# Last batch's second halves written by rows from TensorE, more scaling steps free to change engine, and the whole hand-written order replaced

## Chip, core and metric

The kernel runs on one core of one Trainium2 chip. The metric is the device time of one execution in microseconds (us); the median of the runs is compared. The engines are named as in the profile: PE is TensorE's matmul, PEld its weight load, DVE is VectorE, ACT is ScalarE, POOL is GpSimd, SP is SyncE, which here only issues DMAs. A "q" behind an engine's name means its instruction queue, where DMAs are issued.

## What is computed

The reference has two stages over 8 batches of 576 tokens and 512 channels (8 heads of 64), all in float32:

```python
k_p = k.reshape(B, H, Sp, 8, D).mean(axis=3); v_p = v.reshape(B, H, Sp, 8, D).mean(axis=3)
scores = scale * np.matmul(q, k_p.transpose(0, 1, 3, 2))
attn = exp(scores - max) / (sum + 1e-09)
x = np.matmul(attn, v_p)                       # then heads side by side: (8, 576, 512)
theta = x @ w_theta
y = einsum('ts,bsd->btd', w_tok_r, x * cos(theta)) + einsum('ts,bsd->btd', w_tok_i, x * sin(theta))
u = x + y
out = u + maximum(u @ w_ch, 0.0)
```

The four weight matrices arrive as 64-bit floats (two 32-bit words a number) and are put together on the chip.

## The kernel before, in words

One core does all eight batches. The work is cut into small generators ("streams"), and each `yield` ends a step. A stream's name has a letter for its kind, then the batch, then a part:

- `k`, `v` load keys and values, `K`, `V` pool them, `Q` loads and turns the queries.
- `S b.m` (`soften`, L696) makes the softmax of token tile m: four or eight matmuls (L715, L723), a maximum on DVE, the exponential on ACT (L766 for batches 0 and 1, L778 for the others), the sum and its reciprocal, and then the scaled copy `en` of `e`: one product of 128x512 (L785) and one of 128x64 (L792), on DVE or POOL. POOL takes a product of 512 or more columns in two halves (L172 to L193). From batch 2 on DVE then transposes `en` into `G` (L801, L804), and `E` (`turn`, L856) moves its blocks with 16 DMAs and splits the result in a high and a low part.
- `X` (`attend`, L893) multiplies with the values and copies the result from PSUM into `xT` (L921 on ACT, L923 on DVE).
- `T b.m` (`rotate`, L947) makes theta, its sine and cosine, and the products with x; its cast `xh` (a copy, L204 for ACT, L206 for DVE and POOL) goes to any of three engines.
- `h`, `w`, `c` make the weights. Their words are turned into floats by `to_f32` (L345): the scaled high words always on ACT (L353), the low words on a chosen engine (L357, L359).
- `Z` (`take`, L1013) splits z, and `M b.c.hf` (`mix`, L1034) does the token mixing of channel chunk c and token half hf (288 tokens): 27 matmuls (L1047) in three groups, an addition on DVE (L1057), the cast `uh` (L204, L206) and the low part `ul` (L189 POOL, L1064 DVE).
- `F b.c.hf` (`final`, L1070) is the end of a chunk and half: 12 matmuls (L1080) into a bank `pf`, then `max(.,0)` plus u on DVE (L1087), then a DVE transpose in 32x32 blocks into `R` (L1100), and DMAs to the output. Batches 0 to 6 issue four DMAs a chunk on SP (L1115). Batch 7 issues four DMAs for each of its eight parts (L1105), alternately on ACT's queue and on SP's, from the tile `rz`. Each of these DMAs writes pieces of 32 channels, 128 bytes.

The order is written out by hand: `SCHEDULE` (L30 to L136) is a list of 2064 words. Each word runs one step of the stream that it names (L1198 to L1201), and a letter at its end (v DVE, g POOL, a ACT) is the engine that `pick()` gives in that step. Every engine, and every DMA queue, executes its own instructions in the order in which the words issue them; an engine whose next instruction waits for another engine lets nothing overtake. PSUM has four one-bank buffers for most matmul groups (`bank`, L234) and two double ones. All DMAs of the two queues share eight completion semaphores, and a DMA waits until the earlier one on its semaphore has landed.

At the end of the list PE does the mixing of batch 7, and then the eight `F7` parts one behind the other.

Of the kernel before, what the change touches and what calls it, by code (L numbers as in the profile page):

```python
# [134 lines left out]
F7.1.1 F7.2.0 F7.2.0 F7.0.1 F7.0.1 F7.0.1  # L135
"""  # L136

EARLY, EXACT, V_ON_PE, K_ON_PE, Q_ON_PE, SUMS_ON_ACT = 2, 1, 1, 1, 2, 2


@with_exitstack
def tile_attn_moe(
    ctx: ExitStack,
    tc: tile.TileContext,
# [86 lines left out]
    def bank(shape, name):  # L234
        return ps.tile(shape, F32, tag="mm", name=name, bufs=4)
# [1001 lines left out]
```

## Time and profile before

| what | value |
|---|---|
| median of 3 runs | 571.96 us (570.99 to 573.55) |
| profiled execution, its time | 572.55 us |
| profiled execution, its span from the first to the last instruction | 570.5 us |
| instructions | 11555 |
| mean granted TensorE clock | 0.997 |
| busy: PE, DVE, POOL, ACT | 96%, 80%, 63%, 55% of the span |
| DMA | 57.84 MB, mean 101 GB/s |

The profile page is one profiled execution. Busy time is the union of an engine's instructions; issuing a DMA is not counted as busy. A group's line gives busy time and the mean of one instruction, and behind the bar the idle time of that engine just before these instructions with what ended it. The chain of waits follows the last instruction back to what released it, step by step.

### The profile page before, as it was taken

To read this page: it belongs to the slowest core of one execution; us is meant where nothing else is said; L and a number is where in the kernel's file an instruction comes from. 1 tells how busy PE (TensorE), PEld (TensorE's weight loads), DVE (VectorE), ACT (ScalarE), POOL (GpSimd) and SP (SyncE) were. 2 spreads that over 40 slices of the span, in tenths; PEclk is the share of its full clock that TensorE was granted. 3 is DMA by queue.
4 is the path that set the end of the run, shared out by engine and by line. 5 is a ranking of instruction groups with operands and counts; after the bars stand their busy time and mean duration, and the time that the engine had idled before them with its cause. 6 is when DMAs were issued, how large, how long until landed. Compare 5 with 4: busy or idle time off the path is not lost.

```text
span 570.5 us, 11555 instructions
## 1 busy us (share of the span) xinstructions
PE 546.7 (96%) x4072; PEld 512.9 (90%) x4072; DVE 456.3 (80%) x875; ACT 313.3 (55%) x673; POOL 361.8 (63%) x518
## 2 busy tenths in 40 slices
PE   6999989999999999999999999999999999999993
PEld 5776879998989898999999999999999999999993
DVE  4998998989889999978897997779878775655452
ACT  2999998878554587455417655349225473242000
POOL 3324565687584897648884997838777878522610
PEclk9999999999999999999999999999999999999998
DMA  9995321556676666556565564656234341200225
GB/s 263 270 310 125 81 67 64 120 119 97 131 126 117 127 97 116 105 117 121 109 119 103 84 116 83 122 94 89 41 66 84 66 68 24 44 1 1 43 38 88
DMA packets 235385, 57.84 MB, mean 101 GB/s; under 512 B 223424, under 2 KB 223936, under 8 KB 235328
## 3 DMA queue, kind: packets, MB, share of 16 engines
q1 hardware_dynamic: 230464, 56.52, 50.0%
q10 hardware_dynamic: 4864, 0.59, 0.7%
q8 instruction: 32, 0.52, 0.4%
q14 instruction: 25, 0.20, 0.1%
HBM read 37.81 MB, written 9.44 MB: 83 GB/s over the span
## 4 chain that ended last, share of the span: by engine, by line
PE 65%; DVE 17%; DMA 5%; SPq 5%; POOL 3%; issue 2%; ACT 2%; DVEq 0%; POOLq 0%; ACTq 0%
PE py L1047 27%; PE pf L1080 13%; PE pt L959 11%; PE pv L912 4%; PE s L723 3%; SPq L867 3%; PE px L973 2%; DMA kpst<-in_k_dram 2%; DMA vpst<-in_v_dram 2%; DVE G L801 1%; SPq L603 1%; PE kpp L570 1%; DMA qsst<-in_q_dram 1%; DVE R L1100 1%; DVE en L785 1%
## 5 line engine op out<-in xcount | busy, mean ns | idle before, releaser
L1047 PE MATMUL py<-WTh,zh 128*128 128x288 f32 x576 | 81.9, 288 | 2.8 <-POOL zh L206 2.1
L1047 PE MATMUL py<-WTl,zh 128*128 128x288 f32 x576 | 81.8, 287 | 0.0
L1047 PE MATMUL py<-WTh,zl 128*128 128x288 f32 x576 | 81.3, 289 | 0.2
L1047 PEld LDWEIGHTS py<-WTh,zh 128*128 128x128 f32 x576 | 74.6, 189 | 3.9 <-POOL zh L206 2.3
L1047 PEld LDWEIGHTS py<-WTl,zh 128*128 128x128 f32 x576 | 75.3, 189 | 0.2
L1047 PEld LDWEIGHTS py<-WTh,zl 128*128 128x128 f32 x576 | 74.3, 189 | 1.2 <-DVE zl L1031 0.3
L189 POOL TENSOR_TENSOR zl<-z,zh 128x256 fp32r<-128x256 f32 (+2 forms) x77 | 60.6, 816 | 19.2 <-DVE zh L206 13.5
L189 POOL TENSOR_TENSOR en<-e_eps,ri 128x256 f32<-128x256 f32 (+3 forms) x61 | 34.5, 583 | 48.6 <-DVE ri L782 36.5
L965 ACT ACTIVATE g<-pt,c_magic 128x512 f32<-128x512 f32 x35 | 24.1, 687 | 50.9 <-PE pt L959 34.7
L1057 DVE TENSOR_TENSOR xT<-py,xT 128x288 f32<-128x288 f32 x64 | 27.9, 443 | 25.9 <-PE py L1047 25.6
L1080 PE MATMUL pf<-uh,chh 128*128 128x288 f32 x256 | 43.5, 293 | 1.4 <-DVE xT L923 0.9
L1080 PE MATMUL pf<-ul,chh 128*128 128x288 f32 x256 | 42.1, 286 | 0.2 <-POOL ul L189 0.2
L189 POOL TENSOR_TENSOR ul<-xT,uh 128x288 fp32r<-128x288 f32 x39 | 32.1, 832 | 15.8 <-DVE uh L206 15.5
L1080 PE MATMUL pf<-uh,chl 128*128 128x288 f32 x256 | 41.8, 286 | 0.0
L189 POOL TENSOR_TENSOR xl<-xT,xh 128x256 fp32r<-128x256 f32 x38 | 30.2, 818 | 16.8 <-ACT xh L204 12.5
L1087 DVE SCALAR_TENSOR_TENSOR xT<-pf,xT 128x288 f32<-128x288 f32 x64 | 27.9, 444 | 15.9 <-PE pf L1080 15.6
L778 ACT ACTIVATE e_eps<-e_eps 128x576 f32<-128x576 f32 (+1 forms) x30 | 20.6, 685 | 36.5 <-DVE e_eps L774 36.3
L959 PE MATMUL pt<-th,xh 128*128 128x512 f32 x148 | 39.2, 388 | 0.9 <-ACT xh L204 0.8
L1080 PEld LDWEIGHTS pf<-uh,chh 128*128 128x128 f32 x256 | 36.0, 189 | 2.9 <-DVE xT L923 1.2
L959 PE MATMUL pt<-th,xl 128*128 128x512 f32 x148 | 38.1, 380 | 0.0
L959 PE MATMUL pt<-tl,xh 128*128 128x512 f32 x148 | 38.0, 379 | 0.0
L921 ACT ACTIVATE xT<-pv 128x320 f32<-128x320 f32 (+1 forms) x41 | 15.8, 407 | 38.6 <-PE pv L912 31.1
(259 smaller groups left out, 1441.6 us busy)
## 6 DMA issues: line engine op xcount, KB each, us to landing
out_dram<-R SPq DMA_DIRECT2D x112, 72.0 KB, 2.1
kpst<-in_k_dram SPq DMA_DIRECT2D x15, 512.0 KB, 4.2
vpst<-in_v_dram SPq DMA_DIRECT2D x28, 256.0 KB, 4.0
qsst<-in_q_dram SPq DMA_DIRECT2D x96, 72.0 KB, 2.9
eraw<-G SPq DMA_DIRECT2D x96, 60.0 KB, 2.2
eraw<-G SPq DMA_DIRECT2D x96, 40.0 KB, 2.0
WTh_st<-in_moe_w_theta_dram SPq DMA_DIRECT2D x4, 512.0 KB, 7.5
wcraw<-in_moe_w_ch_dram SPq DMA_DIRECT2D x4, 512.0 KB, 3.5
```

What stands on the lines that cost most here:

```text
L189: nc.gpsimd.tensor_tensor(out[:, r], a[:, r], b[:, r], op)
L723: nc.tensor.matmul(scs[c // 2][:n, 2 * SP * (c % 2) : 2 * SP * (c % 2 + 1)], qT[:, c, t0 : t0 + n], kpT[:, c, :], start=True, stop=True,)
L778: nc.scalar.activation(e[:n], e[:n], AF.Exp, scale=scale)
L867: nc.sync.dma_start(blocks(Ex, jj, i), blocks(Gx, i, jj))
L912: nc.tensor.matmul(as_written(pv[:, :gn]) if pair else pv[:, :gn], l, by_turns(r) if pair else r, start=i == 0, stop=i == len(terms) - 1,)
L921: nc.scalar.activation(x, pv, AF.Copy, scale=1.0 / POOL)
L959: nc.tensor.matmul(as_written(pt), l[:, c, :], by_turns(r[:, c, :]), start=i == 0, stop=i == 11)
L965: nc.scalar.activation(halves(g), in_order(pt), AF.Identity, bias=c_magic)
L1047: nc.tensor.matmul(as_written(py[:, :n]), l[:, kk, :], by_turns(r[:, kk, t]), start=i == 0, stop=i == 3 * NK - 1,)
L1057: nc.vector.tensor_tensor(halves(u), in_order(py[:, :n]), halves(u), ALU.add)
L1080: nc.tensor.matmul(as_written(pv[:, :n]), l[:, kk, o], by_turns(uhl[r][:, kk, t]), start=i == 0, stop=i == 11,)
L1087: nc.vector.scalar_tensor_tensor(halves(oT), in_order(pv[:, :n]), 0.0, halves(oT), ALU.max, ALU.add)
```

## The change

Three functions and the list of words change.

**final.** For batch 7 and the second token half (`BY_ROWS = 1`) the DVE transpose and the four DMAs are gone. In their place PE transposes the 128x288 result in three pieces into a new bank `po` of 96 rows by 3x128, two copies (engine by letter) bring 96x256 and 96x128 to the tile `rows`, and two DMAs write them, in whole rows of 128 channels (512 bytes): the first on SP, the second on SP too, but on ACT's queue for chunk 0. The four DMAs of each first half are now all on ACT's queue.

**soften.** With letter a the large product of `en` is done by eight ACT instructions of 64 columns, each with a scale from `ri` (one number a partition).

**to_f32.** The scaled high words may go to DVE or POOL as well.

```diff
-        nc.scalar.activation(t, hi.bitcast(F32), AF.Copy, scale=2.0**-112)
+        if pick() == "a":
+            nc.scalar.activation(t, hi.bitcast(F32), AF.Copy, scale=2.0**-112)
+        else:
+            ENG[pick()].tensor_scalar(t, hi.bitcast(F32), 2.0**-112, None, ALU.mult)
...
+        if pick() == "a":
+            for h in range(8):
+                nc.scalar.activation(
+                    en[:n, GM * h : GM * h + GM], e[:n, h, 0:GM], AF.Copy, scale=ri[:n, h : h + 1]
+                )
+        else:
+            ENG[pick()].tensor_tensor(
...
+            if hf == BY_ROWS:
+                w = n // 3
+                po = bank([P, 3, P], f"po{c}_{hf}")
+                for j in range(3):
+                    nc.tensor.transpose(po[:w, j], xT[:, c, t0 + w * j : t0 + w * j + w], ident)
+                yield
+                rows = Rs["rows"][:w, c]
+                copy(pick(), rows[:, 0:2], po[:w, 0:2])
+                yield
+                copy(pick(), rows[:, 2], po[:w, 2])
+                yield
+                to = out[b, t, o].rearrange("(j p) a -> p j a", p=w)
+                nc.sync.dma_start(to[:, 0:2], rows[:, 0:2])
+                (nc.sync if c else nc.scalar).dma_start(to[:, 2], rows[:, 2])
+                yield
+                return
...
-                (nc.scalar if i % 2 else nc.sync).dma_start(
+                nc.scalar.dma_start(
```

**SCHEDULE.** All words stand in a new order (2072 of them: the four second halves of batch 7 have two more each), and many letters differ. The ends of the two lists:

```diff
-F7.0.0 M7.2.1v M7.1.1 M7.1.1g M7.1.1v M7.3.1 F7.0.0 F7.3.0 F7.3.0 F7.3.0 M7.3.1g F7.3.0 F7.1.0 F7.1.0 M7.3.1g F7.3.1
-F7.2.1 F7.1.0 F7.0.0 F7.1.1 F7.2.1 F7.3.1 F7.2.1 F7.1.0 F7.2.0 F7.1.1 F7.3.1 F7.1.1 F7.0.0 F7.2.1 F7.2.0 F7.3.1 F7.0.1
-F7.1.1 F7.2.0 F7.2.0 F7.0.1 F7.0.1 F7.0.1
...
+M7.0.1g F7.0.0 F6.0.1 M7.3.1a F7.3.0 M7.3.1g F6.3.1 F7.3.0 F7.1.0 F7.0.0 F7.1.0 F7.2.0 F7.1.0 F7.1.0 F7.2.0 F7.3.1
+F7.2.0 F7.2.0 F7.3.1 F7.1.1 F7.3.1 F7.3.1v F7.3.1v F7.3.1 F7.1.1 F7.2.1 F7.1.1 F7.1.1v F7.1.1v F7.1.1 F7.2.1 F7.0.1
+F7.2.1 F7.2.1v F7.2.1v F7.2.1 F7.0.1 F7.0.1 F7.0.1v F7.0.1v F7.0.1
```

In the new list PE's last groups are, in order: the matmuls of F7.0.0, F7.3.0, F7.1.0, F7.2.0, F7.3.1, F7.1.1, the transposes of F7.3.1, the matmuls of F7.2.1, the transposes of F7.1.1, the matmuls of F7.0.1, the transposes of F7.2.1, and those of F7.0.1. All eight copies of the second halves are on DVE.

How many steps of a kind have each engine, before and after:

| step | DVE | POOL | ACT |
|---|---|---|---|
| large product of `en` (40) | 20, then 15 | 20, then 10 | 0, then 15 |
| cast `uh` (64) | 20, then 18 | 24, then 15 | 20, then 31 |
| low part `ul` (64) | 25, then 22 | 39, then 42 | none |
| cast `xh` (40) | 10, then 7 | 14, then 15 | 16, then 18 |
| high words of the weights (17) | 0, then 5 | none | 17, then 12 |
| copy of `pv` into `xT` (64) | 23, then 21 | none | 41, then 43 |

Read along the words, ACT's exponentials and its sines take turns 34 times in the list before, 30 times in the new one. Matmuls and weight loads of batches 0 to 6 are the same in number and shape.

## Rows read from the trace of the kernel before

**Rows 1.** The page's first part: span, and busy time of each engine.
```profile
span 570.5 us, 11555 instructions
PE 546.7 (96%) x4072; PEld 512.9 (90%) x4072; DVE 456.3 (80%) x875; ACT 313.3 (55%) x673; POOL 361.8 (63%) x518
```

**Rows 2.** Stretches: length, busy PE, PEld, DVE, ACT, POOL; granted clock, DMA share, GB/s.
```profile
0.00:20.00 20.00, 14.78 (x106) 13.60 (x107) 10.70 (x24) 9.84 (x29) 6.16 (x13) 1.00 0.97 285
150.00:200.00 50.00, 46.84 (x358) 44.21 (x359) 45.37 (x86) 25.43 (x45) 32.99 (x44) 1.00 0.69 123
200.00:250.00 50.00, 49.05 (x363) 47.03 (x362) 45.96 (x83) 28.76 (x49) 36.60 (x56) 1.00 0.58 105
300.00:350.00 50.00, 50.00 (x371) 48.50 (x370) 42.38 (x80) 30.16 (x52) 39.11 (x58) 1.00 0.54 102
562.00:570.50 8.50, 0.00 (x0) 0.00 (x0) 0.72 (x2) 0.00 (x0) 0.00 (x0) 0.79 0.56 83
```

**Rows 3.** Waits of PE and PEld: us in total, times, longest us.
```profile
PE kpp L570 <- POOL chh_st L322: 4.6, 1, 4.6
...
PE py L1047 <- POOL zh L206: 2.1, 1, 2.1
...
PEld pv L912 <- ACT xT L921: 2.3, 3, 1.4
```

**Rows 4.** Chain of waits: shares by engine; its last stretch of PE (start, length).
```profile
PE 65%; DVE 17%; DMA 5%; SPq 5%; POOL 3%; issue 2%; ACT 2%; DVEq 0%; POOLq 0%; ACTq 0%
...
549.99 11.77 PE pf L1080 x96
```

**Rows 5.** Issues of line L1105 (min/median/max ns, first and last start), then landing.
```profile
L1105 ACTq DMA_DIRECT2D out_dram<-rz x16: 322/440/478, 554.0 to 563.2; - x16
L1105 SPq DMA_DIRECT2D out_dram<-rz x16: 316/405/472, 558.9 to 568.0; - x16
...
DMA to landing us min/median/max: 1.6/1.7/2.0
```

**Rows 6.** Prices for the end: groups by form, a piece of the chain, one line.
```profile
L1087 DVE SCALAR_TENSOR_TENSOR xT<-pf,xT 128x288 f32<-128x288 f32 x64 | 27.9, 444 | 15.9 <-PE pf L1080 15.6
L923 DVE TENSOR_SCALAR xT<-pv 128x256 f32<-128x256 f32 x12 | 4.8, 416 | 2.9 <-PE pv L912 2.7
...
509.77 0.44 PE px L973 x4
...
L206 DVE COPY kp<-kpp x2: 273/282/292, 8.4 to 12.8; 128x128 f32<-128x128 f32 x2
```

**Rows 7.** Prices for the steps that change engine: groups by line and form.
```profile
L785 DVE TENSOR_TENSOR en<-e_eps,ri 128x512 f32<-128x512 f32 x16 | 13.0, 812 | 0.4
L189 POOL TENSOR_TENSOR en<-e_eps,ri 128x256 f32<-128x256 f32 x28 | 18.0, 666 | 14.3 <-DVE ri L782 8.6 <-DVE mx L757 5.6
L766 ACT ACTIVATE e_eps<-s,mx 128x72 f32<-128x72 f32 x48 | 14.6, 338 | 0.0
L674 ACT COPY vrx<-vrh 32x64 f32<-32x64 f32 x14 | 3.4, 244 | 0.3
L204 ACT CAST uh<-xT 128x288 fp32r<-128x288 f32 x20 | 8.1, 426 | 0.6 <-DVE xT L1057 0.3
L206 POOL CAST uh<-xT 128x288 fp32r<-128x288 f32 x24 | 12.1, 512 | 8.3 <-DVE xT L1057 8.2
L189 POOL TENSOR_TENSOR ul<-xT,uh 128x288 fp32r<-128x288 f32 x39 | 32.1, 832 | 15.8 <-DVE uh L206 15.5
L1064 DVE TENSOR_TENSOR ul<-xT,uh 128x288 fp32r<-128x288 f32 x25 | 14.9, 607 | 0.5 <-POOL uh L206 0.5
L206 DVE CAST xh<-xT 128x512 fp32r<-128x512 f32 x8 | 5.1, 636 | 0.6 <-ACT xT L921 0.5
L353 ACT ACTIVATE wsrc_a<-wraw 128x576 f32<-128x576 f32 x7 | 5.4, 768 | 3.6 <-DMA wraw<-in_moe_w_tok_r_dram 3.5
L359 DVE TENSOR_SCALAR wsrc_b<-wraw 128x576 fp32r<-128x576 uint32 x3 | 1.6, 537 | 0.0
L980 ACT ACT_TABLE_LOAD x16 | 20.5, 1283 | 0.3
```

More of the change, by code (lines that the diff above doesn't have):

```diff
@@ new lines @@
+Q0.0a K0a h1v K0 h1a h1v Q0.1 h0 h1 K0a S0.0 Q0.4 S0.0 Q0.1 Q0.2 h1 Q0.4 w0.1 S0.0 h0g Q0.1a h1g Q0.3 Q0.4v h0 Q0.2v
+w0.1v h0v w0.1g h2 k1.0 S0.1 h0 S0.1 h3 h1 Q0.3 S0.2 S0.0 S0.1 Q0.3v v0.2 h2a D h2v w0.1v S0.1 h2a S0.0 S0.0v S0.0g
+w0.1 S0.3 S0.2 v0.0 S0.1 S0.0 S0.2 K1.0g h1v h1 S0.0v v0.1 S0.1g h3a V0.2 S0.3 h2 w0.1 S0.4 w1.1 h2 S0.0 S0.2 S0.2
+w1.0 S0.3 h3a S0.0v h3v k1.1 S0.1g V0.0 h2v S0.2v S0.3 S0.1 w0.0 S0.2g V0.1 w3.1 S0.1a h3 w2.0 h3 w0.0v w1.1a w3.0
+S0.1 w1.0a S0.1v S0.3 S0.4 w1.0a w0.1g h2 w1.1a w1.0a W0 h2v V0v V0 h2 w1.1a S0.4 Q1.1 S0.2 S0.2a w1.0 X0.0.0 X0.0.1
@@ new lines @@
+T0.2a W1 T0.3a Q1.2 T0.1 W2 Q1.3 w3.1v Q1.2v w4.0v T0.3v V1a c0 T0.2v w4.0a w4.0a T0.1 w4.0 w3.0v Q1.3a T0.2 w4.0 W2a
+Q1.4 X0.2.3g T0.2 T0.1 T0.3 T0.2 W2 c0a c0a T0.2 c0 T0.4g T0.4g T0.2 T0.3 T0.2a w4.0g W3 T0.2 T0.4 W3a T0.3 c0 T0.2
+T0.3 c0 T0.3 T0.2 T0.3a K1 W2 W3 T0.4 T0.4 K1a T0.4 Q1.4 c1 T0.4 c0g W2v T0.3 c0g c0g W2 W4 V1g T0.4 T0.3 c1a T0.4
+T0.3 c1a S1.0 Z0.1a Z0.0g W4v S1.0 k2.2 W4 c1 M0.1.0 Z0.1v c1 K2.2v W4a M0.1.0 M0.0.0 c1 W4 S1.0 W4a S1.0 M0.1.0
+M0.0.0 W4 c2 c1g W4v S1.1 c1g S1.0a W4 Q1.4v c1v W3 W3a Z0.0v W3 M0.1.1 M0.1.1 c2a M0.1.0 S1.0v S1.1 v1.2 M0.0.1 S1.0
@@ new lines @@
+M0.3.1 T1.1g k2.1 Q2.0 S1.3 M0.3.0 T1.0 M0.3.0 S1.3v K2.1g M0.3.1 S1.4 S1.3 M0.2.1a M0.0.1g S1.3 K2 T1.0 M0.2.0g Q2.1
+M0.0.0g M0.3.0 S1.3v T1.0 K2a T1.0a S1.4g T1.0 T1.0 T1.1 S1.3 S1.4v M0.2.1g S1.4 S1.4a T1.0 S1.4 S1.4 M0.1.0g S1.4a
+S1.4 K2 v2.0 V2.0g K2v X1.2.1 T1.1 X1.2.0 X1.2.0a M0.3.0a Q2.1 T1.1 X1.2.2 M0.3.1g X1.2.1a Q2.1 X1.2.3 T1.1 T1.1
+X1.2.2v v2.1 X1.2.3a T1.1v M0.3.0g S2.0 T1.2a S2.0 Q3.0 T1.1 Q3.0 M0.0.1v T1.1 T1.3a T1.2g T1.1 S2.0 V2.1v M0.3.1g
+S2.1 T1.2 S2.2 S2.0 F0.0.1 X1.2.3g T1.2 T1.2 F0.0.1 S2.0g T1.2 S2.0g T1.2 F0.0.0 k3.0 S2.1 S2.1 S2.0 F0.1.0 T1.2a
@@ new lines @@
+S2.3 v3.2 X2.0.0 S2.4 Z1.2g M1.1.0 S2.4 S2.4a Q3.1 V3.0g M1.1.1 M1.0.1 S2.4g X2.0.1 X2.0.1a Q3.1 X2.0.2 V3.2g S3.2
+X2.0.3 S2.4 X2.0.2v Z1.3a X2.0.0a M1.2.0 M1.1.1a M1.3.0 Z1.2g S3.2 S3.2 M1.1.0 F0.3.1 X2.0.3a T2.0a T2.1g S3.2 S3.3
+M1.2.1 M1.2.0 v3.1 M1.0.1a T2.0v S3.2a M1.2.0 Z1.3v E2.2 S3.2v M1.2.0 T2.0 V3.1g M1.2.1 M1.3.0 S3.3 M1.1.0g M1.3.0
+E2.2 M1.2.0v T2.0 S3.3 M1.0.0a M1.3.1 S3.4 T2.1v T2.0 M1.1.0g E2.2 E2.2 T2.0 S3.3 M1.3.1 T2.0 F0.2.1 E2.2a M1.3.0
+T2.0a S3.2 E2.2g k4.0 E2.2g S3.3v S3.3g T2.0 T2.1 M1.2.0g S3.4 E2.2g Q4.0 S3.3 Q4.0 T2.0 k4.2 M1.3.1 S3.4 T2.0 S3.4
@@ new lines @@
+M2.1.1 S4.1a S4.1g X3.0.1a M2.0.0a M2.3.0 M2.3.0 Z2.2a V4.1g S4.1 X3.0.3 Z2.2g X3.0.2 X3.0.3a M2.1.1 S4.2 X3.0.2v
+M2.1.1a S4.2 M2.3.0 T3.0a T3.0g M2.3.1 M2.0.0v M2.3.1 S4.2 M2.1.1v M2.3.1 T3.1a S4.4 V4a T3.0 M2.3.1 k5.0 S4.2g E4.0
+M2.3.0 S4.3 M2.2.1 T3.1g M2.2.0 M2.3.1a E4.0 K5.0v T3.0 S4.2g M2.2.0 T3.2a V4.2g T3.0 M2.3.0a M2.0.1a S4.3 Q5.0 E4.0
+S4.3 M2.1.0g M2.2.1 k5.1 M2.2.0 E4.0 T3.0 k5.2 F1.3.1 T3.2v T3.0 M2.2.1 S4.3 V4g T3.0a Q5.1 S4.2 M2.3.0g T3.0 M2.2.1
+M2.2.1v K5.1g M2.1.0v T3.0 M2.2.0 M2.2.1g v5.0 T3.0 T3.1 T3.4g M2.0.1v Q5.1 K5 V4 T3.1 M2.2.0g T3.1 K5v V4g E4.0g
@@ new lines @@
+F1.2.1 T3.2 T3.1 T3.3a T3.1 K5.2g T3.3g T3.1a M2.3.1v T3.1 F2.1.1 T3.1 T3.1 T3.2 M2.2.0g E4.0a E4.0g F2.1.1 T3.2
+F2.0.1 F2.0.1 F2.1.0 T3.2 T3.2 F2.2.0 Q5.1 T3.2a T3.2 F2.1.0 v5.2 Q6.0 T3.3 S4.3v T3.2 S4.3g K5 T3.2 F2.1.0 F2.0.0
+F2.2.0 S4.4 V5.0g Q6.0 T3.3 F2.1.1 K5a T3.3 T3.3 F2.3.1 T3.3 T3.3a F2.0.0 F2.0.1 T3.3 F2.3.0 S4.4 V4g v5.1 T3.3 E4.0g
+T3.3 Z3.0g F2.2.1 F2.1.1 F2.3.1 Z3.0g F2.0.0 V5.2g F2.0.1 F2.3.0 F2.2.1 M3.0.0 S5.2 F2.3.0 S4.3 X4.0.1 M3.0.1 M3.0.0
+S4.4 S4.4v F2.3.1 F2.2.1 S4.4v F2.2.0 Z3.2a X4.0.0 X4.0.0a S4.4 Z3.2g S5.2 M3.0.1 M3.0.1 V5.1g X4.0.1a X4.0.2 S5.2
@@ new lines @@
+E5.2 T4.0 M3.2.1v M3.2.0g M3.3.0 M3.0.0v T4.0v T4.0 M3.3.1v S5.0 T4.1g M3.0.1v M3.3.0 T4.1 T4.0 M3.3.0v T4.0 M3.1.1g
+M3.3.0g K6 S5.0 T4.1 M3.3.1g F3.0.0 F3.3.0 T4.2v T4.2g X4.2.3g V5a T4.3a T4.1 S5.0 T4.1 S5.0g T4.1 F3.0.0 T4.1a K6v
+F3.3.0 E5.2 E5.2 V5g T4.1 S5.0v Q6.1 T4.1 F3.0.0 V5 T4.1 K6 T4.2 S5.1 E5.2g E5.2g V5v F3.0.1 T4.2 K6v T4.2 F3.1.1
+F3.0.1 F3.1.0 S5.1 T4.3g S5.1 F3.1.0 F3.3.1 F3.0.1 F3.2.1 S5.0 v6.0 F3.3.1 F3.1.1 T4.2 F3.1.0 E5.2g T4.2 V5g T4.2a
+E5.2g T4.3 T4.2 F3.1.1 T4.2 Q6.1 T4.2 X5.2.1 F3.0.1 F3.1.1 T4.3 F3.3.1 S5.1a F3.3.0 Q6.1 S5.1g F3.2.1 T4.3 F3.2.0
@@ new lines @@
+S7.2a M5.1.0 E6.2 V7.0v T6.0a M5.1.0 M5.3.0 V7.2g S7.2v T6.0g M5.1.0 S7.3 M5.0.1v T6.0 S7.3 Z5.2v T6.0 Z5.2v M5.2.0
+T6.1g E6.2 M5.1.0 M5.0.1g T6.0 E6.2 M5.1.1 M5.0.0g E6.2a M5.2.0 E6.2g E6.2g M5.1.0a T6.0 S7.3 T6.0 E6.2v M5.1.0v
+M5.2.1 v7.1 S7.2 T6.0v M5.2.0 T6.0 S7.4 M5.2.1 T6.0 S7.3g F4.2.1 S7.3v M5.2.0 M5.2.0v S7.4 S7.4 M5.3.1 M5.2.1 F4.0.1
+S7.0 T6.0 M5.2.1 X6.2.2 S7.3 M5.2.0g M5.3.0v M5.3.1 X6.2.1 X6.2.1v V7.1g M5.3.1 T6.1g S7.4 M5.2.1g S7.4v X6.2.3
+M5.1.1a S7.4g S7.4 X6.2.2a X6.2.0 T6.1 M5.3.1 M5.3.0v T6.1 X6.2.3a X6.2.0v S7.0 M5.3.1v V7a S7.0 V7g T6.1 F5.1.0 E7.2
@@ new lines @@
+F5.1.0 E7.2 M5.1.1g T6.2g V7 M5.2.1g T6.1 F5.0.0 E7.2 F5.3.0 T6.1 F5.0.0 S7.0 T6.2v T6.3g T6.1a T6.1 F5.1.0 M5.3.1g
+T6.2 F5.0.0 X6.2.3g F5.0.1 F5.3.0 V7g E7.2 F5.1.1 T6.1 T6.1 T6.2 F5.0.1 F5.0.1 F5.0.1 E7.2a T6.2 T6.2 E7.2g F5.1.1
+T6.2 T6.3v F5.2.1 T6.2a F5.2.1 F5.1.1 F5.1.1 T6.3 E7.2g F5.2.0 E7.2g V7v T6.2 F5.2.1 T6.2 T6.2 F5.3.1 F5.2.0 X7.2.2
+F5.2.0 T6.3 T6.3 X7.2.3 F5.3.1 X7.2.1 X7.2.0 F5.3.0 F5.3.1 X7.2.3v T6.3 S7.1 T6.3 X7.2.1v X7.2.2a X7.2.0a T6.3v
+X7.2.3v T6.4v S7.0g T6.3 T6.3 T6.4g T6.3 T6.4 Z6.0g F5.3.1 Z6.0v Z6.0v T6.4 T6.4 T7.3v T6.4 Z6.0g S7.0v T6.4 T6.4a
@@ new lines @@
+T6.4 T6.4 T7.3v M6.0.0 M6.0.1 T6.4 Z6.0a M6.0.0 Z6.0g T7.2a M6.0.1 S7.1 S7.1 M6.0.0 Z6.1g T7.3 M6.0.1 F5.2.1 Z6.1g
+S7.0 M6.0.0 S7.1 S7.1v S7.1g M6.1.0 M6.0.0 M6.0.1 M6.1.0 S7.1 E7.0 M6.1.0 M6.0.0a M6.1.1 M6.1.1 E7.0 M6.1.1 Z6.3g T7.3
+M6.0.1 M6.1.0 M6.3.0 M6.1.1 Z6.3g Z6.2g M6.0.0v M6.3.1 M6.3.0 M6.2.0 M6.2.0 Z6.2v T7.3 E7.0 E7.0 M6.2.0 M6.3.1 T7.2g
+M6.2.0 T7.4g M6.3.1 M6.1.1a M6.3.0 M6.3.0 T7.3 M6.2.1 M6.3.1 T7.3 M6.0.1g T7.3a E7.0a M6.2.1 M6.1.1v E7.0a E7.0v
+M6.2.1 M6.3.1v T7.3 T7.3 M6.2.1 E7.0g M6.2.0a M6.3.1g M6.2.1a T7.2 M6.0.1g X7.0.1 T7.3 X7.0.0 X7.0.1v X7.0.2 T7.2
@@ L136 @@
 """
 EARLY, EXACT, V_ON_PE, K_ON_PE, Q_ON_PE, SUMS_ON_ACT = 2, 1, 1, 1, 2, 2
+BY_ROWS = 1
 @with_exitstack
@@ L784, in soften @@
         en = temp(b, m, "en", 8 * SP)
[L785 to L790 removed]
+        if pick() == "a":
[5 more added lines that the diff above has]
+            ENG[pick()].tensor_tensor(
+                en[:n, 0:512].rearrange("p (h g) -> p h g", h=8),
+                e[:n, :, 0:GM],
+                ri[:n].unsqueeze(2).broadcast_to([n, 8, GM]),
+                ALU.mult,
+            )
         yield
@@ L1094, in final @@
                 Rs["z"] = rz[:, 0 : NC * S].rearrange("p (c s) -> p c s", c=NC)
+                Rs["rows"] = rz[:, NC * S : NC * S + 12 * P].rearrange("p (c j a) -> p c j a", c=4, j=3)
             R = Rs["z"][:, c]
+            if hf == BY_ROWS:
[14 more added lines that the diff above has]
+                return
         else:
```

161 lines of the change are left out of this document (53 added, 108 removed).

## The prediction, made before the changed kernel was run

> **What bounds the kernel now.** I read the page's busy times first, then the stretches, the waits of PE, the chain of waits, and last the DMA issues of the end. The reader is to see in the busy times that PE is the bound: 546.7 of 570.5 us [rows 1]. The 23.8 us that it is not busy are the most that any order of the same work can give back, and they lie in three places. At the start PE's first matmul waits 4.6 us [rows 3]; k0.0 and K0.0 head both lists, so I leave that alone. At the end PE's last group closes at 549.99 + 11.77 = 561.76 us [rows 4], and 8.7 us follow in which it does nothing [rows 1, 2, 4]. What is left, 23.8 - 4.6 - 8.7 = 10.5 us, are short waits in the body, the longest 2.1 us before the first mixing [rows 3]. Most of them lie before 250 us: in 150 to 250 us PE lacks 4.1 of 100 us while DVE is busy for 91% of the time; in 300 to 350 us PE lacks nothing [rows 2]. The chain says the same: 65% PE, 17% DVE, 3% POOL, 2% ACT [rows 4]. So DVE, where it matters, is the engine that PE waits for directly or through others.
>
> **The end, removed part by part.** After the last PE group DVE needs two instructions, but SP issues DMAs of the last batch from 558.9 until 568.0 us, 16 of them, some 0.5 us apart near the end, while ACT's queue has issued its own by 563.2 us [rows 5]. The last lands 1.7 us after its issue, at 569.7, and 0.8 us of closing waits bring the span to 570.5. So the end is bound by SP's queue. The change takes 16 issues of the second halves down to 8 and gives SP 7 of these; the 16 of the first halves go to ACT's queue.
>
> Is ACT's queue late instead? Its first part is F7.3.0. The new list puts six more matmul groups of 1.47 us (11.77 / 8) and six transposes between that part's matmuls and the end of the last group, some 9.5 us; four DVE steps of 0.46 us stand before the first DMA, so it can be issued about 7.6 us before PE's last group ends. Sixteen at 0.5 us are through 0.4 us after that end, ahead of the one issue of F7.0.1, which comes 2.9 us after it. I cost it at nothing; the cover is 2.5 us. SP has by then the eight issues that remain of batch 6 and six of the second halves, and stands free before the last.
>
> **The end, added.** T is the end of the last matmul group. Three transposes take 3 x 0.11 = 0.33 us of PE [rows 6] and end some 0.16 us later, so 0.5 us. Two copies from PSUM cost DVE 0.42 us (by the 128x256 copy) and 0.28 us (by the 128x128 copy) [rows 6]. After T come the transposes of F7.2.1 0.5, its two copies 0.70, the DVE step of F7.0.1 0.44, its transposes 0.5, its copies 0.70, six handovers of some 0.03, the last DMA 1.7 from issue to landing, and the close 0.8: 5.5 us. Before T PE has six transposes more, 0.7 us, with 0.1 us for changing shapes. The end is then 0.8 + 5.5 = 6.3 us instead of 8.7: **-2.4 us**. On the small side, every second half waits on DVE: after a matmul group DVE still has two copies, and then the step of the next part, about 1.8 us against 1.8 us of PE work; if each of two such places loses 0.5 us and the landing takes 2.0 us, -1.1 us is left. On the large side, copies and handovers at half their price give -3.2 us. No row has a landing of 512-byte rows; it takes the 1.6 to 2.0 us of the 128-byte ones [rows 5]. The clock is no term here: it was granted in full to 562 us, and its mean of 0.79 stands in the stretch after PE had stopped [rows 2].
>
> **Steps that change engine.** Fifteen large products of `en` go to ACT, eight instructions each. No row shows one. The nearest is the exponential on 72 columns with a number a partition, 338 ns [rows 7], of which 14.6 / 48 = 0.305 us is its own busy time; a copy of 64 columns without such a number is 244 ns. So a block costs ACT between 8 x 0.244 = 2.0 and 8 x 0.338 = 2.7 us; I take 8 x 0.305 = 2.4, the row nearest in operands, in all 36 us. A block on DVE took 0.81, on POOL 2 x 0.67 = 1.33 us. By the Trainium skill ("ScalarE: Activation LUTs", What ACT_TABLE_LOAD costs), an instruction with one pointer operand takes 280 ns + 0.833 ns a column, and neighbours overlap by 93 ns: an estimate of 8 x 333 - 7 x 93 = 2.0 us a block and 30 us in all, the lower end of my bounds.
>
> - ACT: +36 for `en`, +11 x 0.43 for `uh`, -5 x 0.77 for high words, and four table loads fewer at 1.28 [rows 7]: 36 + 4.7 - 3.8 - 5.1 = +32 us on 313, to 60% of the span. Its idle time hides nearly all of it; 10% on its 2% of the chain is 1.1 us.
> - DVE: -5 x 0.81 for `en`, -3 x 0.61 for `ul`, -2 x 0.5 for `uh`, -3 x 0.64 for `xh`, +5 x 0.54 for high words [rows 7]: -6.1 us on 456, 1.3%, and of its 17% of the chain (97 us) -1.3 us.
> - POOL: -10 x 1.33, -9 x 0.51, +3 x 0.83 [rows 7]: -15 us on 362, 4%; on 3% of the chain (17 us) -0.7 us.
>
> Together **-0.9 us** in the body. The unlettered rest is small in number, and I leave it out. The redrawn order moves loads and DMA issues past others on SP's queue too; of PE's longest waits none in the body names a DMA [rows 3], so I cost that at nothing, and a load that comes late would show as a new wait of the second rival's kind. This term is the uncertain one. Its bound below is the whole 10.5 us of the body's waits; its bound above is the third rival.
>
> **Sum.** -2.4 - 0.9 = -3.3 us. The profiled execution took 572.55 us, 2.05 us more than its span, so it comes to 569.25 us. It stands 0.6 us above the median of the runs; against 571.96 us the forecast is **568.7 us**, 0.6% faster. Half a per cent, 2.9 us, is about what a measurement of this kernel can tell from no change.
>
> **Rivals.**
>
> First, **the body gains more.** If the relief of DVE and the four table loads less remove half of the body's waits, 5.2 us instead of 0.9, the time is 571.96 - 2.4 - 5.2 = 564.4 us. For it speaks that DVE is at 91% where PE waits [rows 2]; against it, that these waits are many and short, each with another cause.
>
> Second, **the gain of the end is spent in the body.** A new order has new places in which PE's next group waits. One more wait as before the first mixing, 2.1 us [rows 3], takes nearly all of the 2.4 us, and without the 0.9 the time is 571.7 us. For it speaks that the work and its engines hardly change, and that three engines' orders were redrawn at once; this leaves between 570 and 574 us.
>
> Third, **slower: ACT's blocks hold up the PSUM buffers.** PE has four one-bank buffers, and ACT empties most `pv` and all theta banks. A block keeps ACT for 2.4 us in which a bank that is full stays full; PE already waits for ACT's copies of `pv` three times, up to 1.4 us [rows 3]. If half of the 15 blocks stand before such a copy and each costs PE 1 us, that is 7 us: 571.96 - 2.4 + 7 = 576.6 us. It decides from 5.3 us of new waits on. ACT's idle time speaks against it: it is busy for 57% of 200 to 250 us [rows 2]. The rule that stands behind this rival is that of the Trainium skill ("ScalarE: Activation LUTs", Rules for kernel authors), to do element-wise products on VectorE and not on ScalarE. The trace agrees as far as the price goes, 2.4 against 0.81 us.
>
> **How the numbers follow.** The forecast has 0.43, its own range 566.5 to 571 us by the bounds of the end and a body of +0.5 to -2; two thirds of it are faster by over 0.5%. The first rival has 0.22, the second 0.20, the third 0.15. Faster: 0.29 + 0.22 = 0.51. Within: 0.14 + 0.20 = 0.34. Slower: 0.15. The range reaches from the first rival, 564.0, past the second into the third, 574.5 us.
>
> **What would show each step.** After the change, PE's last `pf` group should close near 561.7 us (561.76 + 0.8 - 0.9) and the span some 5.5 us later; the last issue should be ACT's single one of `rows`, and ACT's 16 should be through before it. The DVE transposes of `rz` should be four, the copies of `po` near 0.42 and 0.28 us. An `en` block on ACT should last 2.0 to 2.7 us, and DVE should be busy for some 450 us, ACT for some 345. Waits of PE on ACT's copies well above 2.3 us would be the third rival. An end of over 7.6 us, or a last issue still queued behind others, would make the first term wrong; PE waits in the body of more than 10.5 us, or of less than 7, the second.

## The result and the profile after

| | before | after |
|---|---|---|
| median of the runs | 572.26 us, 4 runs (570.99 to 573.55) | 567.27 us, 4 runs (565.27 to 568.15) |
| profiled execution: time, span | 572.55, 570.5 us | 568.15, 566.3 us |

The ratio is 0.9882, 95% interval 0.9853 to 0.9910: faster by 1.2%. A second comparison gave 0.9898 (0.9872 to 0.9924). The forecast was 568.7 us in a range of 564.0 to 574.5.

The page's first part (busy time of each engine; compare [rows 1]):

```profile
span 566.3 us, 11646 instructions
PE 546.2 (96%) x4084; PEld 515.1 (91%) x4084; DVE 455.6 (80%) x867; ACT 330.6 (58%) x774; POOL 373.2 (66%) x526
```

ACT has 17 us more work, POOL 11 us more, DVE 1 us less. I had forecast about +32, -15 and -6, so the relief that was to make the body faster did not come as busy time.

PE up to the end of its last group, in the kernel before and in the changed one (length; busy PE, PEld, DVE, ACT, POOL; granted clock, DMA share, GB/s):

```profile
0.00:561.76 561.76, 546.66 (x4072) 512.90 (x4072) 455.41 (x873) 313.32 (x673) 361.82 (x518) 1.00 0.51 102
```

```profile
0.00:561.07 561.07, 545.37 (x4080) 514.74 (x4081) 453.97 (x862) 330.62 (x774) 373.21 (x526) 1.00 0.51 102
```

Without the wait at the start (4.6 and 5.0 us) PE is idle in the body for 561.76 - 546.66 - 4.6 = 10.5 us before and for 561.07 - 545.37 - 5.0 = 10.7 us after.

The chain of waits at the end (start, length, what):

```profile
559.60 1.47 PE pf L1091 x12
561.07 0.34 PE po L1112 x3
...
561.44 0.62 DVE rz L208 x2
562.05 0.38 DVE xT L1098
...
562.57 0.52 PE po L1112 x3
...
563.11 0.42 DVE rz L208
```

The last `pf` group ends at 561.07 us, and 566.3 - 561.07 = 5.2 us follow, where 8.7 followed before. The last group stands 0.7 us earlier than before [rows 4], although six transposes of some 0.11 us now lie ahead of it. So of the 4.2 us that the span lost, 3.5 - 0.7 = 2.8 belong to the end and 0.7 + 0.7 = 1.4 to the body.

The waits of PE (us in total, times, longest us; compare [rows 3]):

```profile
PE kpp L575 <- DMA kpst<-in_k_dram: 5.0, 1, 5.0
PE pv L923 <- ACT xT L932: 2.4, 2, 1.9
PE py L1058 <- ACT zh L206: 1.7, 1, 1.7
PE po L1112 <- DVE xT L1098: 1.2, 1, 1.2
```

The wait of 1.9 us in the second row is new. The stretches show where it lies and what it hides, first one of the kernel before, then those of the changed kernel:

```profile
250.00:300.00 50.00, 50.00 (x389) 47.59 (x388) 43.51 (x80) 23.71 (x42) 42.01 (x59) 1.00 0.64 119
```

```profile
150.00:200.00 50.00, 49.34 (x381) 47.52 (x380) 41.92 (x77) 34.97 (x84) 43.35 (x63) 1.00 0.69 127
200.00:250.00 50.00, 48.92 (x372) 46.35 (x371) 42.56 (x80) 33.31 (x78) 39.55 (x54) 1.00 0.53 101
250.00:300.00 50.00, 48.08 (x362) 46.22 (x361) 40.55 (x72) 23.83 (x41) 40.08 (x58) 0.97 0.65 120
...
285.50:287.42 1.92, 0.00 (x0) 0.00 (x1) 1.92 (x4) 0.44 (x2) 1.76 (x4) 1.00 0.00 0
...
289.00:292.00 3.00, 3.00 (x14) 3.00 (x14) 2.06 (x6) 1.75 (x4) 0.00 (x0) 0.50 0.41 68
```

Between 150 and 250 us PE lacks 1.7 us instead of 4.1 [rows 2]. But from 250 to 300 us, where it lacked nothing, it now lacks 1.9: at 285.5 us it stands for 1.92 us, and soon after that the granted clock is 0.50 (1.2 of 2.4 GHz) for some 3 us. The timeline there (start, length, what; in brackets idle time and what ended it):

```profile
281.96 3.09 POOL L191 TENSOR_TENSOR zl<-z,zh 128x384 fp32r<-128x384 f32 x4
281.97 4.53 DVE L803 TENSOR_TENSOR en<-e_eps,ri 64x64 f32<-64x64 f32 x1
...
285.02 2.20 POOL L191 TENSOR_TENSOR vpst<-vpst 128x256 f32<-128x256 f32 x3
286.43 0.46 DVE L1128 STREAM_TRANSPOSE R<-xT 128x288 f32<-128x288 f32 x1
...
286.98 0.66 ACT L932 ACTIVATE xT<-pv 128x256 f32<-128x256 f32 x2 [9.00 <-DVE R L1128]
...
287.42 0.38 PE L923 MATMUL pv<-eh,Vh 128*128 128x256 f32 x1 [1.92 <-ACT xT L932]
...
288.42 4.05 PE L1058 MATMUL py<-WTh,zl 128*128 128x288 f32 x18
```

One product of 64 columns holds DVE for 4.53 us; instructions of its line take 0.175 us at the least. Meanwhile POOL runs products without a pause. Behind it on DVE stands a transpose of `xT`, behind that an eviction on ACT, and behind that PE. This became the main question for the experiments: the new order gains more in the body than the sum shows and gives some of it back here.

### The profile page after: what moved, and what is told of

Same layout as the page of the kernel before. It is cut to its first block, busy times and chain, and to the rows that moved or that the text cites. A ratio compares the mean times of both kernels' runs of the same rounds, so it can differ in the third digit from the quotient of the medians.

```text
span 566.3 us, 11646 instructions
## 1 busy us (share of the span) xinstructions
PE 546.2 (96%) x4084; PEld 515.1 (91%) x4084; DVE 455.6 (80%) x867; ACT 330.6 (58%) x774; POOL 373.2 (66%) x526
## 4 chain that ended last, share of the span: by engine, by line
PE 66%; DVE 10%; DMA 8%; SPq 6%; POOL 4%; issue 3%; ACT 1%; DVEq 0%; POOLq 0%; ACTq 0%
PE py L1058 32%; PE pt L970 12%; PE pf L1091 11%; PE pv L923 4%; PE s L728 3%; PE px L984 2%; DMA kpst<-in_k_dram 2%; SPq L878 2%; DMA WTh_st<-in_moe_w_theta_dram 2%; DMA wraw<-in_moe_w_tok_r_dram 2%; DMA vpst<-in_v_dram 1%; SPq L608 1%; DMA out_dram<-R 1%; SPq L629 1%; DVE en L803 1%
## 5 line engine op out<-in xcount | busy, mean ns | idle before, releaser
L1058 PE MATMUL py<-WTh,zl 128*128 128x288 f32 x576 | 83.0, 292 | 0.0
L191 POOL TENSOR_TENSOR zl<-z,zh 128x256 fp32r<-128x256 f32 (+2 forms) x80 | 63.5, 825 | 22.3 <-ACT zh L206 13.2
L1058 PEld LDWEIGHTS py<-WTh,zl 128*128 128x128 f32 x576 | 76.2, 193 | 0.1
L191 POOL TENSOR_TENSOR ul<-xT,uh 128x288 fp32r<-128x288 f32 x42 | 34.0, 823 | 22.1 <-DVE uh L208 12.2
L728 PE MATMUL s<-kpT,qT 128*128 128x144 f32 x256 | 36.9, 288 | 1.9 <-ACT kpT L206 0.8
L792 ACT ACTIVATE en<-e_eps,ri 128x64 f32<-128x64 f32 (+1 forms) x120 | 30.3, 335 | 13.3 <-DVE ri L787 9.5
L762 DVE TENSOR_REDUCE mx<-s 128x8 f32<-128x576 f32 (+2 forms) x42 | 29.9, 715 | 9.6 <-PE s L728 9.4
L728 PEld LDWEIGHTS s<-kpT,qT 128*128 128x128 f32 x256 | 33.6, 190 | 3.1 <-issue 1.1
```

Source lines behind the costliest of these rows:

```text
L191: nc.gpsimd.tensor_tensor(out[:, r], a[:, r], b[:, r], op)
L728: nc.tensor.matmul(scs[c // 2][:n, 2 * SP * (c % 2) : 2 * SP * (c % 2 + 1)], qT[:, c, t0 : t0 + n], kpT[:, c, :], start=True, stop=True,)
L762: nc.vector.tensor_reduce(mxv, scv, AX.X, ALU.max)
L792: nc.scalar.activation(en[:n, GM * h : GM * h + GM], e[:n, h, 0:GM], AF.Copy, scale=ri[:n, h : h + 1])
L1058: nc.tensor.matmul(as_written(py[:, :n]), l[:, kk, :], by_turns(r[:, kk, t]), start=i == 0, stop=i == 3 * NK - 1,)
```

## The experiments

Each was compared in five rounds with the kernel before; the ratios are to that kernel. Two theories stood at the start: the end and the body give what the two traces say (2.8 and 1.4 us), or one of them gives everything.

**1. The new body with the old end.**

```diff
-BY_ROWS = 1
+BY_ROWS = -1
-                nc.scalar.dma_start(out[b, t, ch0 ...
+                (nc.scalar if i % 2 else nc.sync).dma_start(out[b, t, ch0 ...
```

and without the two extra words of each F7 second half.

> The changed kernel with the output of batch 7 written out as in the kernel before (no transposes on TensorE for the second half, output issues alternating between the two queues); order and engines of everything else as changed. Theory (the end gives about 2.9 us of the 4.2 us, the body the rest): the last group of pf ends about 0.7 us earlier than the changed kernel's 561.07, some 8.7 us lie behind it, and the time is about 2.9 us above the changed kernel's, 1.5 to 2 us under the kernel before (ratio about 0.997). Rival (the end gives nothing and the redrawn body everything): no change against the changed kernel, ratio about 0.988 to the kernel before.

570.55 us, ratio 0.9958 (0.9928 to 0.9988). Its chain ends

```profile
552.90 5.40 PE pf L1088 x44
...
558.33 0.47 DVE xT L1095
```

and its span at 566.9 us, 8.6 us behind the last group (558.30). SP's queue is late again: 14 of its issues lie between 558.03 and 564.85 us. The group ends 2.8 us earlier than in the changed kernel, where 0.7 were expected; the profiled execution is the fastest of the nine, and in it the clock did not fall behind the stall, which is there with 2.0 us at 284 us. The body alone, stall included, is worth 0.4%, some 2.4 us (0.7 to 4.1).

**2. The old body with the new end.** The code of the change with the words and engines of before; only the words from the first `F7.0.0` on are the new ones.

> The kernel before, its order and engines as they were up to the last feed-forward blocks of batch 7; only the end of batch 7 is rewritten to the changed kernel's (rows from TensorE, all second-half issues late on their queues). Theory: 2.4 to 2.9 us under the kernel before (ratio 0.995 to 0.996), with about 5.2 us behind the last group of pf. Rival (the end gives nothing): ratio 1.000. Second rival (the end gives everything, the body nothing): ratio about 0.988, as the whole change.

571.42 us, ratio 0.9944 (0.9921 to 0.9968), 3.2 us (1.8 to 4.5). The last group ends at 563.24 us and the span at 568.5: 5.3 us, where 5.2 were expected. The two halves together, 0.56% and 0.42%, make 0.98%; the whole change is worth 1.0 to 1.2%. So end and body add up within the noise, some 0.3% on each, and neither gives everything.

**3. One letter.**

```diff
-S4.4 S4.4v F2.3.1 F2.2.1 S4.4v F2.2.0
+S4.4 S4.4v F2.3.1 F2.2.1 S4.4g F2.2.0
```

> The changed kernel with one letter of the order changed: the small product of en of one attention block (the sixth step of S4.4) goes from VectorE to GpSimd. In the changed kernel's profile it took 4.53 us on VectorE while GpSimd ran products one after the other, TensorE stood for 1.92 us behind it and then ran 3 us at a granted clock of 0.50. Theory (that instruction is what stalls TensorE, and the low clock follows from the stall): no VectorE instruction of over 2 us at that place, no wait of TensorE of over 0.5 us there, no stretch of granted clock 0.50 behind it; 1.9 + 1.5 = about 3.4 us less than the changed kernel's profile, about 2 to 3.5 us in the median (ratio to the kernel before about 0.983). Rival (the next VectorE instruction with two operands in SBUF is held up in its place, or GpSimd gets late for Z): the stall stays or moves, time within 0.5 us of the changed kernel's.

563.97 us, ratio 0.9815 (0.9787 to 0.9842); by the ratios 3.8 to 4.8 us below the changed kernel (0.9882 and 0.9898 in its two comparisons), more than the 2 to 3.5 expected, with some 2 us of doubt on either figure (the medians differ by 3.3). The timeline at the same place:

```profile
282.68 0.29 POOL L191 TENSOR_TENSOR en<-e_eps,ri 64x64 f32<-64x64 f32 x1
...
286.05 0.27 PE L923 MATMUL pv<-eh,Vh 128*128 128x256 f32 x1
...
286.94 2.37 PE L1058 MATMUL py<-WTh,zl 128*128 128x288 f32 x18
```

No wait is left, and the 18 matmuls take 2.37 us where they took 4.05. In its profile PE comes to the first of the rows 1.4 us earlier than in the changed kernel's (286.05 against 287.42 us), and is 3.2 us ahead once those matmuls are through. A product of 0.29 us on POOL replaces one of 4.53 us on DVE.

**4. The same product, with a pause on POOL.** Experiment 3 takes the product from DVE; it does not show what held it. Here it stays on DVE, and POOL's step `V5.1g`, the products of `vpst` that ran behind those of `zl`, moves behind `Z3.1g`.

> The changed kernel with one step of GpSimd's (the products of vpst, three of them, then vp) moved behind its next products of zl, so that GpSimd has a pause of some microseconds after the four products of zl; the small product of en stays on VectorE. Theory (VectorE's product is held up until GpSimd leaves a gap between its products): it still starts with the first product of zl, ends with the fourth, and so takes about 3.1 us instead of 4.53; TensorE's wait behind it falls from 1.92 us to about 0.5 us, and the low clock behind it goes; ratio to the kernel before about 0.983. Rival (the product waits for something of its own, its operands or ScalarE): 4.5 us and the wait of 1.9 us stay, ratio 0.988.

```profile
281.21 3.07 POOL L191 TENSOR_TENSOR zl<-z,zh 128x384 fp32r<-128x384 f32 x4
281.22 3.14 DVE L803 TENSOR_TENSOR en<-e_eps,ri 64x64 f32<-64x64 f32 x1
...
285.27 0.38 PE L923 MATMUL pv<-eh,Vh 128*128 128x256 f32 x1 [0.53 <-ACT xT L932]
...
296.20 0.52 POOL L191 TENSOR_TENSOR vp<-vpst 128x128 f32<-128x128 f32 x1
296.75 0.40 SPq L519 DMA_DIRECT2D kpst<-in_k_dram  x1
...
297.20 3.28 SPq L878 DMA_DIRECT2D eraw<-G  x5
...
306.67 0.71 DVE L812 STREAM_TRANSPOSE G<-en 128x512 f32<-128x512 f32 x1 [7.68 <-DMA eraw<-G]
...
312.57 0.60 PE L923 MATMUL pv<-eh,Vh 128*128 128x320 f32 x1 [2.34 <-DVE xT L1068]
```

The product took 3.14 us and ended with the fourth product of `zl`; PE's wait fell to 0.53 us. That is the theory to a tenth of a microsecond: it is POOL's products that hold it, and nothing of its own. That it takes a pause of POOL to let it through is not shown; the last section has a case against it. The time missed: 573.30 us, ratio 0.9998 (0.9977 to 1.0020). The rows show where the gain went. POOL's `vp` is done only at 296.72 us, and 0.03 us later SP issues a load that stood at 291.30 us in the changed kernel. The moves of `eraw` stand behind it on SP's queue, DVE waits 7.68 us for one of them, and PE then waits 1.9 and 2.3 us for DVE. Behind these waits the clock is at 0.50 from 312.2 to 319.0 us, which costs some 3 us more. I had costed POOL's step as if nobody waited for its buffer.

**5. The ScalarE blocks undone.** 15 letters go back, as `S1.0a` to `S1.0v`, `S3.0a` to `S3.0g`.

> The changed kernel with the 15 blocks of products of en that it gives to ScalarE put back on the engines that they had before (7 on VectorE, 8 on GpSimd); nothing else undone. Theory (the ScalarE blocks relieve VectorE and GpSimd, which is where the body's 1.35 us come from): VectorE and GpSimd busy for some 10 and 12 us more, TensorE waits more, the time is 1 to 2 us above the changed kernel's. Rival (the ScalarE blocks hold up the evictions and cost time, and other steps of the redrawn order pay for it): the time is 1 us or more below the changed kernel's. If it is within 0.5 us, the blocks are off the chain either way.

579.60 us, ratio 1.0084 (1.0054 to 1.0113): 10.7 to 11.6 us above the changed kernel, where the theory had 1 to 2. The largest new place, in the timeline of this kernel:

```profile
361.52 2.22 POOL L191 TENSOR_TENSOR en<-e_eps,ri 128x256 f32<-128x256 f32 x2 [3.60 <-ACT zh L206]
363.71 2.21 POOL L191 TENSOR_TENSOR vpst<-vpst 128x256 f32<-128x256 f32 x3
...
366.73 0.28 POOL L208 CAST zh<-z 128x128 fp32r<-128x128 f32 x1
...
367.06 0.39 PE L1058 MATMUL py<-WTh,zh 128*128 128x288 f32 x1 [2.73 <-POOL zh L208]
```

and the same steps in the changed kernel:

```profile
353.96 0.28 POOL L208 CAST zh<-z 128x128 fp32r<-128x128 f32 x1
...
355.12 2.02 ACT L792 ACTIVATE en<-e_eps,ri 128x64 f32<-128x64 f32 x8
```

With the block on POOL, POOL first waits 3.60 us, then multiplies, then does the values' products, and a cast of 0.28 us that PE needs stands behind all of it. With the block on ACT the cast is done before the block even starts. After PE's wait the clock falls here too (0.51 from 368.1 to 371.6 us). In the body of this profile it stands at 0.50 for three stretches of 3.4 us, in the changed kernel's for one. At 217 us it is the same: a block of 1.22 us on POOL stands ahead of `Vr`, and PE waits 1.89 instead of 0.7 us.

**6. The ScalarE blocks alone**, in the order of before and with its end.

> The order of the kernel before with its old end; only the 15 blocks of products of en that the change gives to ScalarE go to ScalarE. Theory (the blocks are worth something only with the order drawn around them, since putting them back cost 12 us in the new order): between 1 us faster and 3 us slower than the kernel before, ratio 0.998 to 1.005. Rival (the blocks relieve VectorE and GpSimd wherever they stand): 2 us or more faster than the kernel before, ratio under 0.9965. Second rival (ScalarE's blocks hold up the evictions where the order was not drawn for them): 4 us or more slower, ratio over 1.007.

583.92 us, ratio 1.0176 (1.0132 to 1.0221): the second rival. One of its four waits of PE of about 2 us, the stretch and the timeline there:

```profile
PE pv L920 <- ACT xT L929: 2.3, 1, 2.3
```

```profile
150.00:200.00 50.00, 44.95 (x359) 42.84 (x358) 39.09 (x80) 34.46 (x81) 29.40 (x41) 1.00 0.66 118
```

```profile
170.99 2.02 ACT L789 ACTIVATE en<-e_eps,ri 64x64 f32<-64x64 f32 x8
172.91 0.36 ACT L929 ACTIVATE xT<-pv 128x256 f32<-128x256 f32 x1
```

DVE is relieved by some 6 us of 50 (45.4 in [rows 2]), and yet PE lacks 5.1 us there where it lacked 3.2. The copy of `pv` that PE waits for stands behind a block of 2.02 us on ACT. The clock is at half for some 10 us of this profile (from 223.4 to 230.3 and from 264.4 to 267.8 us), so about 5 us of the loss are its. Blocks without the order cost 10.1 us, the order without the blocks (experiment 5) costs 4.8 us even with the new end; both together gain 2.4 us with the old end.

**7. High words back on ScalarE** (`h0`, `h1`, `w0.1`, `w2.0`, `w4.0`).

> The changed kernel with the scaled high words that it has on VectorE (h0, h1, w0.1, w2.0, w4.0) back on ScalarE; nothing else undone. Theory (they lie beside other work, five pieces of under 1 us): within 1 us of the changed kernel, ratio 0.986 to 0.990. Rival (ScalarE is late in the first 100 us and the five pieces were on TensorE's path): 1 to 3 us above the changed kernel, ratio 0.991 or more.

568.12 us, ratio 0.9901 (0.9869 to 0.9933): no difference that can be measured from 0.9882 and 0.9898. This part of the change is hidden either way.

**8. A shorter end, with the letter.** The `max` of the last part moves ahead of the copies of the part before it, which go to ACT:

```diff
-F7.2.1 F7.2.1v F7.2.1v F7.2.1 F7.0.1 F7.0.1 F7.0.1v F7.0.1v F7.0.1
+F7.2.1 F7.0.1 F7.2.1a F7.2.1a F7.2.1 F7.0.1 F7.0.1v F7.0.1v F7.0.1
```

> The changed kernel with the one letter of e3_one_letter (the small product of en to GpSimd) and, at the end, the closing step of the last block on VectorE ahead of the copies of the block before it, which go to ScalarE. Theory: TensorE's wait of 1.1 us for VectorE before the last transposes goes, the span ends about 4.1 us behind the last group of pf instead of 5.2, and the time is about 1.1 us below e3_one_letter's (ratio to the kernel before about 0.9795). Rival (ScalarE's copies of po are slow enough, or its issue late enough, that the end stays at its queue): no change against e3_one_letter, ratio 0.9815.

564.26 us, ratio 0.9838 (0.9806 to 0.9870). PE's wait of 1.1 us fell to 0.2, but 4.9 us remain behind the last group, 0.3 less instead of 1.1: SP's queue issues the last three DMAs from 558.22, 558.63 and 559.13 us, one behind the other, the last 0.4 us after its data. The median cannot be told from experiment 3.

**9. The same, with one issue moved to ACT's queue**, beside the changed kernel once more.

```diff
-(nc.sync if c else nc.scalar).dma_start(to[:, 2], rows[:, 2])
+(nc.sync if c % 2 else nc.scalar).dma_start(to[:, 2], rows[:, 2])
```

> The changed kernel once more, for a comparison on the same chip with e9_two_queues: ratio to the kernel before 0.988, by its first comparison 0.985 to 0.991, the wait of 1.9 us behind the small product of en at 285 us and, in most executions, the low clock behind it. If the wait were a chance of one execution, it would be gone here.

> The kernel of e8_letter_and_end with one more step: of the last block but one the second piece of the output is issued by ScalarE's queue and not by the synchronisation engine's, whose last issue stood 0.4 us behind its data there. Theory (the end is bound by that queue again): last issue 0.4 us earlier, 4.5 us from the last group of pf to the end of the span where the changed kernel has 5.2; with the letter 3 to 5 us below the changed kernel (ratio to the kernel before about 0.981, and to the changed kernel about 0.993). Rival (the landing, not the issue, sets the end): 4.9 us behind the last group, as in e8_letter_and_end.

The changed kernel took 567.25 us, 0.9898 (0.9872 to 0.9924), this one 563.22 us, 0.9834 (0.9807 to 0.9861), 0.65% less. The last group of its chain is

```profile
555.29 1.49 PE pf L1091 x12
```

and its span ends at 561.4 us, 4.6 us behind that group (4.5 were expected). Among experiments 3, 8 and 9 the medians are too near to choose; by the shape of the end this is the one to keep.

## Why the prediction was right, and where not

- **Where the time lies.** PE as the bound, the end of 8.7 us and the short waits before 250 us were read rightly: experiments 1 and 2 find the gain in the end and in the body, and they add up; in the trace PE lacks 2.4 us less between 150 and 250 us.
- **The end, -2.4 us.** Right in its mechanism. It measured 2.8 us in the profile and 3.2 (1.8 to 4.5) alone. Behind the last group lie 5.2 us where I had 5.5. The copies were 0.42 and 0.28 us as taken, but together 0.62, since they overlap. ACT's 16 issues were through ahead of the single one. The rows of 512 bytes landed 1.8 to 2.0 us after their issue (medians of the two kinds on SP), where I had taken the 1.7 of the 128-byte pieces. The place on the small side, that DVE has the `max` behind two copies, is there too: PE waits 1.2 us for it.
- **The price of a block on ACT.** I took 2.4 us; it is 30.3 / 15 = 2.0 us, the lower bound. The estimate from the Trainium skill ("ScalarE: Activation LUTs", What ACT_TABLE_LOAD costs) was 2.0 us, and the trace agrees: 30.3 us for 120 instructions of 335 ns each.
- **The engines' sums: this step failed.** "The unlettered rest is small in number, and I leave it out": it was not. POOL's groups, first the changed kernel's, then before's:

```profile
L191 POOL TENSOR_TENSOR kpst<-kpst 128x256 f32<-128x256 f32 x33 | 24.8, 766 | 5.2 <-DMA kpst<-in_k_dram 2.5 <-issue 1.2 <-DVE er L846 0.6
L191 POOL TENSOR_TENSOR en<-e_eps,ri 128x64 f32<-128x64 f32 (+3 forms) x37 | 23.3, 642 | 13.3 <-DVE ri L787 5.8 <-DVE G L815 3.1 <-ACT er L206 3.1
```

```profile
L189 POOL TENSOR_TENSOR en<-e_eps,ri 128x256 f32<-128x256 f32 (+3 forms) x61 | 34.5, 583 | 48.6 <-DVE ri L782 36.5 <-DVE mx L757 5.6 <-DVE G L804 3.0
L189 POOL TENSOR_TENSOR kpst<-kpst 128x256 f32<-128x256 f32 x21 | 16.5, 802 | 3.5 <-DMA kpst<-in_k_dram 2.8
```

  `en` gave POOL 11 us back, but the pooling of the keys, 12 products of `kpst` among them, and other steps went to it. Of the 15 us that ACT has less than forecast, 6 are the cheaper blocks; most of the rest are copies and casts of other kinds that left it (of `xr`, `eh`, `qT` and more).
- **The body, -0.9 us: mis-sized, by a way of pricing that does not hold.** It measured 1.4 us in the trace and 2.4 us (0.7 to 4.1) by experiment 1. I multiplied busy time by an engine's share of the chain. Experiments 5 and 6 show that the same 15 blocks cost 10 us in one order and save 11 us in the other. By the places read there, what decides is which short step stands behind a block on its in-order queue, not how busy the engine is. The prediction's own sign speaks against this term too: PE's waits in the body are 10.7 us, above the 10.5 that I had set, 1.9 of them the stall. The last group ends earlier all the same because PE is busy for 1.3 us less before it, although six more transposes (0.7 us) and 1.7 us lost to the half clock are in that time; why its matmuls took less time was not looked for.
- **Luck.** That the time came out 1.4 us from the forecast is in part luck. The body's 1.4 us in the trace are what is left of some 4.5 us that it gains without the stall at 285 us (the first rival, below), and neither that gain nor the stall stood in the sum.
- **The first rival** (the body gains 5.2 us) was nearer than I gave it: without the stall at 285 us the body gains 2.4 + 3.8 = 6.2 us by the ratios of experiments 1 and 3, with some 3 us of doubt. By the trace of experiment 3, whose last group ends at 557.91 us, it gains 561.76 - 557.91 + 0.66 = 4.5 us, the 0.66 being the six transposes. **The second rival** is that stall: a wait of 1.9 us and the clock behind it took the difference back. **The third rival**, ACT's blocks ahead of PSUM copies, is what happens in the old order (experiment 6) and does not happen in the new one. Its rule, products on VectorE (the Trainium skill, "ScalarE: Activation LUTs", Rules for kernel authors), agrees with the rows on price, 2.0 us on ACT against 0.81 on DVE [rows 7]; on time the measurement says the opposite here, since putting them back on VectorE and GpSimd costs 11 us.
- **Left open.** What brought the other waits of experiments 5 and 6 was read from their traces, place by place, and not undone one by one. The order was not tried apart from the other letters that changed with it (`uh`, `ul`, `xh`, the keys). How much the new order would gain with its letters chosen again was not tried beyond one letter.

## What to carry to other kernels

Where one engine is busy for 96% and the others follow hand-written in-order queues, price a moved step by what stands behind it on the queue that it joins, and by whose buffer or DMA it releases; its own duration and the load of the engine say little. A change of engines and the order drawn for it are one edit: measure them apart only to learn, not to keep half. After such a change look for single instructions that take many times the least duration of their line; here one letter at such a place was worth as much as the whole end.

## What was unexpected in the hardware

- **A short VectorE product can be held up by a run of GpSimd products.** 4.53 us in the changed kernel and in three others with the same neighbours (4.51 to 4.54 us), 3.14 us when the run was four products long, 0.18 us at the least. It started within 0.01 us of the first product of `zl` and there it ended with the first pause. The kernel before has a milder case, which got through without one:

```profile
169.11 3.09 POOL L189 TENSOR_TENSOR zl<-z,zh 128x384 fp32r<-128x384 f32 x4
169.27 2.32 DVE L792 TENSOR_TENSOR en<-e_eps,ri 64x64 f32<-64x64 f32 x1
```

  It ends at 171.59 us, while POOL's four products run on until 172.20 us; in experiment 6 the same product beside the same four took 0.41 us. So POOL's products hold it, and the runs do not settle at which of their ends it gets through. The Trainium skill ("SBUF — State Buffer", Who interferes with whom) says that a VectorE instruction with two inputs in SBUF and a GpSimd one that reads SBUF use a shared port in turn, the second to come waiting for the first. The traces agree that it waits; but at 285 us it waited for six products, not for one.
- **The clock fell after a wait of under 2 us, but not each time.** In the changed kernel's profile PE stood for 1.92 us, ran for over a microsecond at 1.00 and was then at 0.50; the 18 matmuls there took 4.05 us instead of 2.37. In the second comparison's profile the same wait (1.93 us) was followed by 1.00:

```profile
285.50:287.60 2.10, 0.17 (x3) 0.03 (x1) 2.10 (x4) 0.46 (x2) 1.94 (x4) 1.00 0.00 0
...
289.00:292.00 3.00, 2.45 (x26) 2.12 (x27) 2.16 (x6) 1.59 (x4) 0.00 (x0) 1.00 0.37 62
```

  A wait of 1.73 us near 76 us stands in nine of the profiles; behind it the clock fell in three, those of experiments 4, 5 and 7 (0.50 for 3.4 us each), and not in the other six. So such a wait costs its own length or nearly twice that, which fits how the executions of one kernel differ: of the changed kernel's first four, three had a mean clock of 0.996 and took 566.9 to 568.2 us, one had 1.000 and took 565.3.
